# Experts with tokens as the moving operand: one store of y per item, zero rows behind each expert, and a conversion spread over seven items

## The chip, the cores and the metric

The kernel runs on one core of a Trainium2 chip. The metric is the device time of one execution in microseconds; lower is better. Five engines have a queue of their own: TensorE (PE in the rows; PEld are its weight loads), VectorE (DVE), ScalarE (ACT), GpSimd (POOL) and SyncE (SP), which computes nothing here and issues most DMAs. An instruction that waits holds up all that stand behind it on its engine.

## The reference

A chain of three parts, cut to what matters; arrays are fp32 but for w_in and w_out, which come as fp64:

```python
x = attention(q, k, v)               # 4608 tokens x 512
logits = norm(x) @ norm(emb).T / tau # 8 experts
idx = argmax(logits); gate = softmax(logits)[idx]
for e in range(8):
    m = idx == e
    out[m] = gate[m] * (relu(x[m] @ w1[e]) @ w2[e])   # 512 -> 1024 -> 512
h = out @ w_in                       # 512 -> 2048
y = (h * cos(h)) @ w_out             # 2048 -> 512
```

With these inputs the experts get 42, 708, 1, 145, 0, 2242, 1018 and 452 tokens.

## The kernel before

**Precision.** Each fp32 operand is split into a high and a low part (hi, lo), and a product is three matmuls: hi*hi, hi*lo, lo*hi. So each weight and each x needs a copy on ScalarE (hi) and a subtraction on VectorE or GpSimd (lo).

**Attention (0 to 186 us).** It makes x tile by tile, chooses the expert of each token, and GpSimd scatters the rows (with the gate as an extra column) into xv in DRAM, where each expert has a region of its own (`scatter`). `zero_rows` writes one block of zeros, the first 128 rows of each region, at step ZR = 8.

**Experts (to 898 us).** The work is a list of items: a wide item is up to 512 tokens of one expert, a narrow one up to 256. The table `tab` holds for each item its rows in xv, its columns in yv and the place of its weights; it is computed on VectorE during item 0 (`tables`). With these inputs there are 8 wide and 5 narrow items. Items 0 to 4 always run; wide items from 5 on and the narrow ones stand in nested If blocks on counts. Tokens are the moving operand: weights are loaded as 128x128 blocks and x, transposed, streams through.

An item has 16 steps k. Steps 0 to 7 are `gemm1(k)`: 12 matmuls into one of two banks, ScalarE's relu (L752) to hi, VectorE's L753 to lo. Steps 8 to 15 are halves of `gemm2`, whose result ScalarE copies to ys (L768). Beside them run for the next item: the loads of its x rows (`x_load`, L729, four of 257 KB), the multiplication by the gate (`gate`, L734, ScalarE), transposes on TensorE (`t_x`, L739) with XHI (L741, ScalarE) and XLO (L742, VectorE), its weights (`fetch`: four loads of 512 KB for w1 at L123 or w2 at L119, each after SP has read the address from `tab`), and their split (L126 ScalarE, L129 GpSimd or VectorE). The dictionaries FIRST, WIDE and NARROW say at which step each of these stands. At the item's end `y_store` writes ys to yv in four stores of 128 tokens (two in a narrow item); the first two of a wide item are declared disjoint, the others wait for the landing of the earlier ones.

**Conversion.** The feed-forward weights are converted from fp64 bits to fp32 in 32 pieces, each one load into one of two buffers craw, seven VectorE ops (L839 to L853) and one store wd<-co (L854) from the one buffer co; the sixth op, L849, is the first to write co. They are spread over items 0 to 4 by `conv`. In items 1 to 4 GpSimd also scatters each token's position to pv (`pos_scatter`, nine in each).

**Feed-forward (898 us to the end).** 9 groups of 512 tokens by 16 steps, with the converted weights read back and split (`f_load`, `f_split`), x read from yv (`x2_load`, `x2_split`), and the result scattered to the tokens' places. `prepare` does the first of these during the first narrow item.

All engines' orders are those in which the code is written.

## Time and profile before

| | us |
|---|---|
| median of 3 runs (1723.82 to 1728.4) | 1724.88 |
| the profiled execution's own time | 1710.43 |
| its span | 1708.5 |
| attention | 0 to 186 |
| item 0 | 216.1 to 284.2 |
| items 1 to 4 | 284.2 to 603.8 |
| wide items 5, 6, 7 | 603.8 to 757.5 |
| five narrow items | 757.5 to 898.3 |
| feed-forward | 898.3 to the end |

The stages' bounds are the starts of TensorE's first gemm of each. TensorE is busy for 1468.2 us of the span, VectorE for 924.8, ScalarE for 609.7, GpSimd for 490.9. The sum over the span tells little: the stages have different limits, so the windows by item, the waits and the timelines are read.

### The profile page before, as it was taken

The page shows a single profiled execution, that of the slowest core. Times are in us where ns is not written, and L with a number is a line of the kernel's source. Part 1 is how long each engine was busy: PE and PEld are TensorE (multiplying, and loading weights), DVE is VectorE, ACT ScalarE, POOL GpSimd, SP SyncE. Part 2 cuts the span into 40 slices and gives each one's busy share as a digit, 9 for nine tenths or more (in the row PEclk, how much of TensorE's full clock was granted, in tenths as well). Part 3 has the DMA queues.
Part 4 walks back from the last instruction along what each step waited for, and adds up shares of the span by engine and source line. Part 5 has one row for each costly group of instructions (what it writes and reads, how often), then busy time and mean ns, then how long its engine had stood idle before and what let it go on. Part 6 is the DMA issues. An engine that isn't in the chain of part 4 may idle for free. (4 is left out here: it accounts for less than half of the span.)

```text
span 1708.5 us, 20626 instructions
## 1 busy us (share of the span) xinstructions
PE 1468.2 (86%) x7480; PEld 1240.5 (73%) x7480; DVE 924.8 (54%) x1616; ACT 609.7 (36%) x1006; POOL 490.9 (29%) x378
## 2 busy tenths in 40 slices
PE   5999378384738579978998999999999999999996
PEld 4999256273636458868996788888888888888885
DVE  5788446373635431114446875656565656565653
ACT  5898324131212233326553332323232323232321
POOL 5576424242425224426333420202020202020200
PEclk9999689697969789999999999999999999999998
DMA  9973617464444554336663210101010101010000
GB/s 267 258 200 115 210 40 221 115 197 133 145 140 144 160 171 137 117 120 219 226 224 111 87 50 1 50 1 50 1 50 1 50 1 50 1 50 1 25 0 25
DMA packets 107073, 177.77 MB, mean 104 GB/s; under 512 B 16584, under 2 KB 54472, under 8 KB 106960
## 3 DMA queue, kind: packets, MB, share of 16 engines
q1 hardware_dynamic: 99888, 157.38, 30.6%
q0 software_dynamic: 6912, 18.94, 3.0%
q8 instruction: 62, 1.02, 0.2%
q14 instruction: 51, 0.42, 0.1%
q10 hardware_dynamic: 160, 0.02, 0.0%
HBM read 135.87 MB, written 40.43 MB: 103 GB/s over the span
## 5 line engine op out<-in xcount | busy, mean ns | idle before, releaser
L129 POOL TENSOR_TENSOR lo<-raw,hi 128x1024 fp32r<-128x1024 f32 x84 | 201.0, 2398 | 433.1 <-ACT hi L126 377.2
L749 PE MATMUL ph<-xhi,hi 128*128 128x512 f32 (+1 forms) x416 | 104.9, 377 | 139.9 <-DVE hb L753 116.7
L919 ACT ACTIVATE ys<-ph,quarter 128x512 f32<-128x512 f32 x144 | 99.0, 688 | 297.2 <-PE ph L911 297.2
L749 PEld LDWEIGHTS ph<-xhi,hi 128*128 128x128 f32 x416 | 73.7, 203 | 157.0 <-DVE hb L753 119.2
L935 PE MATMUL po<-fh,xhi 128*128 128x512 f32 x576 | 179.3, 392 | 3.2 <-DVE xhi L925 2.2
L935 PE MATMUL po<-hi,xhi 128*128 128x512 f32 x576 | 179.5, 391 | 0.4 <-DVE xhi L925 0.2
L922 ACT ACTIVATE ys<-ys 128x512 f32<-128x512 f32 x144 | 91.0, 632 | 227.5 <-DVE ys L921 227.5
L925 DVE TENSOR_TENSOR xhi<-ys,xhi 128x512 fp32r<-128x512 f32 x144 | 157.6, 1094 | 5.1
L923 DVE TENSOR_TENSOR ys<-ys,ph 128x512 f32<-128x512 f32 x144 | 99.2, 689 | 100.5 <-ACT ys L922 100.5
L920 DVE TENSOR_SCALAR co<-ys 128x512 f32<-128x512 f32 x144 | 62.7, 436 | 158.6 <-ACT ys L919 158.6
L764 PE MATMUL py<-ha,hi 128*128 128x256 f32 (+1 forms) x576 | 141.7, 338 | 2.0 <-ACT ha L752 1.9
L935 PEld LDWEIGHTS po<-fh,xhi 128*128 128x128 f32 x576 | 108.8, 189 | 27.3 <-DVE xhi L925 3.4
L935 PEld LDWEIGHTS po<-hi,xhi 128*128 128x128 f32 x576 | 108.1, 188 | 26.0 <-DVE xhi L925 3.4
L126 ACT ACTIVATE hi<-raw 128x1024 fp32r<-128x1024 f32 x108 | 112.2, 1053 | 12.9 <-SPq L998 8.7
L749 PE MATMUL ph<-xlo,hi 128*128 128x512 f32 (+1 forms) x416 | 103.8, 375 | 13.8 <-DVE xlo L742 13.8
L935 PE MATMUL po<-fl,xhi 128*128 128x512 f32 x288 | 112.6, 391 | 0.0
L935 PE MATMUL po<-lo,xhi 128*128 128x512 f32 x288 | 112.2, 390 | 0.0
L764 PEld LDWEIGHTS py<-ha,hi 128*128 128x128 f32 x576 | 97.2, 192 | 11.3 <-ACT ha L752 2.1
L921 DVE TENSOR_TENSOR ys<-ys,co 128x512 f32<-128x512 f32 x144 | 99.7, 693 | 4.9
L897 POOL TENSOR_TENSOR hb<-craw,hb 128x1024 fp32r<-128x1024 f32 x10 | 25.6, 2555 | 264.8 <-ACT hb L896 264.8
L749 PE MATMUL ph<-xhi,lo 128*128 128x512 f32 (+1 forms) x416 | 99.5, 363 | 2.4 <-POOL lo L129 2.4
L764 PE MATMUL py<-ha,lo 128*128 128x256 f32 (+1 forms) x288 | 95.9, 333 | 0.0
(201 smaller groups left out, 2862.0 us busy)
## 6 DMA issues: line engine op xcount, KB each, us to landing
raw<-in_moe_w_dram SPq DMA_DIRECT2D x116, 512.0 KB, 5.8
xr<-xv SPq DMA_DIRECT2D x46, 257.0 KB, 3.2
yv<-ys SPq DMA_DIRECT2D x42, 256.0 KB, 4.1
kraw<-in_k_dram SPq DMA_DIRECT2D x12, 768.0 KB, 9.2
vraw<-in_v_dram SPq DMA_DIRECT2D x8, 1152.0 KB, 7.6
craw<-yv SPq DMA_DIRECT2D x9, 1024.0 KB, 5.5
q<-in_q_dram SPq DMA_DIRECT2D x8, 1024.0 KB, 12.7
craw<-in_moe_w_in_dram SPq DMA_DIRECT2D x16, 512.0 KB, 4.3
```

What stands on the lines that cost most here:

```text
L126: nc.scalar.activation(HI[c], RAW[c], AF.Copy)
L129: eng.tensor_tensor(LO[c], RAW[c], HI[c].bitcast(F32), ALU.subtract)
L749: nc.tensor.matmul(p[:, 0:w], W[kk][:, f * 128:(f + 1) * 128], x[:, kk, 0:w], start=(c == 0), stop=(c == 3 * KC - 1))
L764: nc.tensor.matmul(p[:, 0:w], W[4 + f // 2][:, o:o + 128], h_at(f, m, w), start=(f == 0 and c == 0), stop=(f == FC1 - 1 and c == 2))
L897: nc.gpsimd.tensor_tensor(x[:, t, :], raw, x[:, s, :].bitcast(F32), ALU.subtract)
L919: nc.scalar.activation(u, p, AF.Identity, scale=1.0 / TWO_PI_EXACT, bias=quarter)
L920: nc.vector.tensor_scalar(nr, u, MAGIC, MAGIC, op0=ALU.add, op1=ALU.subtract)
L921: nc.vector.tensor_tensor(u, u, nr, ALU.subtract)
L922: nc.scalar.activation(u, u, AF.Sin, scale=TWO_PI)
L923: nc.vector.tensor_tensor(u, u, p, ALU.mult)
L925: nc.vector.tensor_tensor(gl, u, gh.bitcast(F32), ALU.subtract)
L935: nc.tensor.matmul(O[g][r], a[:, r * 128:(r + 1) * 128], wf(f, s, 1), start=(f == 0 and c == 0), stop=(f == FC2 - 1 and c == 2))
```

## The change

- **y_store:** one store of the whole item (512 or 256 columns), whose columns run on beyond the expert's end; the next item's store overwrites them. Each item needs one address instead of two or four.
- **Zero rows:** no longer the first rows of each region before the scatters, but 128 rows right behind each expert's last token, in eight stores with addresses from `basei`, issued by SP in item 0 (step 4) before the rows of item 1 are loaded. Rows of an item beyond its tokens point to them through `tab`.
- **w1:** the fetch for the item after next moves from the end of an item to step 14, except in item 0. For item 0 itself the w2 fetch moves behind the x rows. The first two items' row loads wait for the last eight scatters or zero stores issued ahead of them (`behind`).
- **Start:** the last chunk's routing, its scatters and the tables' set-up stand ahead of item 0's gates; the four gates come in a row, then four transposes in four banks. `tables` has 52 VectorE ops, 12 in each of steps 0 to 4 instead of steps 3 to 7.
- **Conversion:** two buffers co, and 3, 5, 5, 5, 5, 5, 4 pieces in items 0 to 6 instead of 32 in items 0 to 4. If item 5 or 6 does not run, Else branches do its pieces. In item 0 the pieces stand in steps 10 to 15.
- **Feed-forward's preparation:** spread over steps 0 to 15 of the first narrow item; f_split(1) stands right before the feed-forward loop; the buffers for split weights are laid out anew.

```diff
-    yv = dram.tile([128, KC, REG + 128], F32, name="yv")
+    yv = dram.tile([128, KC, NT + 512], F32, name="yv")
...
@@ -204,7 +212,6 @@
             lambda: V.tensor_scalar(m, k, float(REG), None, op0=ALU.mult),
             lambda: V.tensor_scalar(tab0[:, 0:4], row4, m[:, 0:1], None, op0=ALU.add),
             lambda: fetch(tab0, 0, 4, 0),
-            lambda: fetch(tab0, 0, 4, 1),
         ]
 
...
@@ -727,14 +738,16 @@
             for r in range(n):
                 row = nc.sync.value_load(t[i:i + 1, r:r + 1], min_val=0, max_val=E * REG - 128)
                 d = nc.sync.dma_start(xr[r], xv[bass.ds(row, 128), :])
+                if r == 0 and i < 2:
+                    behind(d, SENT[-8:])
                 if t is tab0:
                     tc.add_to_no_dep_group("xv_rows", d.ins)
...
-        def t_x(r):
-            p = bank(0, "ptx")
+        def t_x(r, b=0):
+            p = bank(b, "ptx")
             for kk in range(KC):
...
-        def y_store(i, n, k):
-            y = ys_at(n * 128)
-            for r in range(n):
-                col = nc.sync.value_load(tab[i:i + 1, 4 + r:5 + r], min_val=0, max_val=NT)
-                d = nc.sync.dma_start(yv[:, :, bass.ds(col, 128)], y[:, :, r * 128:(r + 1) * 128])
-                if r < 2 and n == 4:
-                    apart(f"y{k}", d)
+        def y_store(i, w):
+            col = nc.sync.value_load(tab[i:i + 1, 4:5], min_val=0, max_val=NT)
+            nc.sync.dma_start(yv[:, :, bass.ds(col, w)], ys_at(w))
+
+        def zero_rows(zeros):
+
+            for e in range(E):
+                row = nc.sync.value_load(basei[0:1, e:e + 1], min_val=e * REG, max_val=e * REG + NT)
+                d = nc.sync.dma_start(xv[bass.ds(row, 128), :], zeros)
+                apart("xv_rows", d)
+                SENT.append(d)
...
+        def item(i, w, conv=None, mid=None, when=None):
 
             n = w // 128
             w1c, w2c, on_dve, gates, txs = when
@@ -790,7 +809,9 @@
                 x_load(tab, i + 1, n)
             for k in range(16):
                 if k == 8:
-                    fetch(tab, i + 1, 8, 1)
+                    fetch(tab, i + 1, 5, 1)
+                if k == 14 and i:
+                    fetch(tab, i + 2, 5, 0)
                 if k < 8:
                     gemm1(k, w)
...
-                    conv(i, k)
+                    conv(k)
                 if k < 8:
                     for r in gates.get(k, ()):
                         gate(r)
-            fetch(tab, i + 2, 8, 0)
-            y_store(i, n, key)
-
-        FIRST = {11: (0,), 12: (1,), 13: (2,), 14: (3,)}, {1: (4, 5, 6, 7)}, (), {10: (0, 1), 12: (2, 3)}, {11: (0,), 12: (1,), 14: (2,), 15: (3,)}
+            if not i:
+                fetch(tab, 2, 5, 0)
+            y_store(i, w)
+
+        FIRST = {12: (0,), 13: (1,), 14: (2,), 15: (3,)}, {1: (4, 5, 6, 7)}, (1, 3), {11: (0,), 12: (1,), 13: (2,), 14: (3,)}, {12: (0,), 13: (1,), 14: (2,), 15: (3,)}
         WIDE = {8 + k: (k,) for k in range(4)}, {k: (4 + k,) for k in range(4)}, (), {4 + k: (k,) for k in range(4)}, {9: (0,), 11: (1,), 13: (2,), 15: (3,)}
...
+            o = co[j % 2]
...
+        PART = [3, 5, 5, 5, 5, 5, 4]
+        assert sum(PART) == 2 * FC2
+
+        def conv_part(i, k0, k1):
+
+            if i >= len(PART):
+                return None
+            j0, n = sum(PART[:i]), 7 * PART[i]
+            g = (x for j in range(j0, j0 + PART[i]) for x in conv_one(j))
+
+            def some(k):
+                for _ in range(n * (k - k0 + 1) // (k1 - k0) - n * (k - k0) // (k1 - k0) if k0 <= k < k1 else 0):
+                    next(g)
+            return some
...
         while todo and todo[0] < EARLY:
             scatter(todo.pop(0))
         x_load(tab0, 0, 4)
+        fetch(tab0, 0, 4, 1)
+        f1, f2 = route(NTILE - CHUNKS[-1], NTILE, const, lambda: bank(6, "pr"))
+        while todo:
+            scatter(todo.pop(0))
+        for f in f1:
+            f()
         for c in range(4):
             w_hi(c)
             w_lo(c, nc.vector)
+        for f in f2:
+            f()
+        for i in range(NTILE - CHUNKS[-1], NTILE):
+            scatter(i)
+        zeros = second_part()
+        late = tables(co[0], craw[0][:, 0, :])
         for r in range(4):
             gate(r)
-            t_x(r)
-        f1, f2 = route(NTILE - CHUNKS[-1], NTILE, const, lambda: bank(6, "pr"))
-        while todo:
-            scatter(todo.pop(0))
-        for f in f1[:-1]:
-            f()
-
-        late = []
+        for r in range(4):
+            t_x(r, (0, 3, 4, 5)[r])
 
         def mid0(n):
-            if n == 2:
-                f1[-1]()
-                for f in f2:
+            if n < 8:
+                for f in late[:LATE]:
                     f()
-                for i in range(NTILE - CHUNKS[-1], NTILE):
-                    scatter(i)
-                second_part()
-                late.extend(tables(co[0], craw[0][:, 0, :]))
-            if 2 < n < 8:
-                for f in late[:12]:
-                    f()
-                del late[:12]
-                if not late and not X1:
-                    X1.append(1)
-                    fetch(tab, 1, 8, 0)
+                del late[:LATE]
+                if not late and zeros is not None and not once:
+                    once.append(1)
+                    zero_rows(zeros)
                     x_load(tab, 1, 4)
+                    fetch(tab, 1, 5, 0)
                     conv_load(0)
                     conv_load(1)
 
-        X1 = []
-        item(0, 512, 0, conv, mid0, FIRST)
+        once = []
+        item(0, 512, conv_part(0, 10, 16), mid0, FIRST)
+        assert once
         for i in range(1, NW0):
...
         def more_wide(i):
-            with tc.If(nw > i):
-                item(i, 512, i, None, None, WIDE)
+            with tc.If(nw > i) as c:
+                item(i, 512, conv_part(i, 0, 16), None, WIDE)
                 if i + 1 < NWM:
                     more_wide(i + 1)
+            if i < len(PART):
+                with c.Else():
+                    for j in range(i, len(PART)):
+                        conv_part(j, 0, 1)(0)
 
...
         def prepare(k):
-            if k < 2:
-                x2_split(0, k)
-            if k == 2:
+            if k == 0:
+                f_load(0)
+            if k == 8:
+                x2_load(0)
+            if k == 10:
                 f_split(0)
+            if k in (13, 14):
+                x2_split(0, k - 13)
+            if k == 15:
                 for f in range(1, 4):
                     f_load(f)
-            if k == 6:
-                f_split(1)
 
         def more_narrow(j):
             with tc.If(nn > j) as c:
-                item(NROW + j, 256, 100 + j, None, (lambda k: prepare(k - 8) if k >= 8 else None) if not j else None, NARROW)
+                item(NROW + j, 256, None, None if j else prepare, NARROW)
                 if j + 1 < E:
                     more_narrow(j + 1)
             if not j:
                 with c.Else():
-                    for k in range(8):
+                    for k in range(16):
                         prepare(k)
 
         more_wide(NW0)
-        x2_load(0)
-        f_load(0)
         more_narrow(0)
...
         WF.extend((HI[c], LO[c]) for c in range(8))
-        WF.extend((piece(ffw, f"fh{f}"), piece(ffw, f"fl{f}")) for f in range(12, FC2))
+        WF.extend((piece(ffw, f"fh{f}"), piece(ffw, f"fl{f}")) for f in range(11, FC2 - 1))
+        WF.append(tuple(XLO[:, 2 * i:2 * i + 2, :].rearrange("p a n -> p (a n)") for i in range(2)))
+        f_split(1)
```

**SP, the end of item 1.** The rows stand between item 1 and item 2: raw are pieces of a later item's w1, yv<-ys the stores of y, xr the rows of x, wd the conversion's store. Before (the four rows of L773 and L774 stand there four times in a row, and so do those of L728 and L729):

```order
L123 DMA raw_109<-in_moe_w_dram 128x1024
L773 TENSOR_LOAD tab
L773 ISA x2
L774 REGISTER_ALU
L774 DMA yv<-ys 512x1x128
...
L728 TENSOR_LOAD tab
L728 ISA x2
L729 ISA
L729 DMA xr_101<-xv 128x514
...
L854 DMA wd<-co 128x512
```

And in the changed kernel:

```order
L124 DMA raw_110<-in_moe_w_dram 128x1024
L784 TENSOR_LOAD tab
L784 ISA x2
L785 REGISTER_ALU
L785 DMA yv<-ys 512x1x512
L739 TENSOR_LOAD tab
L739 ISA x2
L740 ISA
L740 DMA xr_102<-xv 128x514
...
L875 DMA wd<-co_2642 128x512
```

One store with one address stands where four did, the row loads come right behind it, and the w1 loads ahead of it are now issued at step 14.

**SP, in item 0, the rows of item 1.** tab_92 and tab_93 are the small table of item 0, tab that of all items; craw is the conversion's load. Before:

```order
L729 DMA xr_104<-xv 128x514
L116 TENSOR_LOAD tab
L116 ISA x2
L123 ISA
L123 DMA raw_106<-in_moe_w_dram 128x1024
...
L728 TENSOR_LOAD tab
L728 ISA x2
L729 ISA
L729 DMA xr_101<-xv 128x514
...
L826 DMA craw<-in_moe_w_in_dram 128x4x256
```

And in the changed kernel (the four rows of L790 and L791 stand there eight times):

```order
L120 DMA raw_114<-in_moe_w_dram 128x2x512
L790 TENSOR_LOAD basei
L790 ISA x2
L791 ISA
L791 DMA xv<-zeros 128x514
...
L739 TENSOR_LOAD tab
L739 ISA x2
L740 ISA
L740 DMA xr_102<-xv 128x514
...
L124 DMA raw_107<-in_moe_w_dram 128x1024
...
L848 DMA craw<-in_moe_w_in_dram 128x4x256
```

Eight zero stores now stand ahead of the rows of item 1, and the w1 fetch stands behind these rows instead of ahead of them.

## Rows read from the trace of the kernel before

**Rows 1.** The page's head and its busy totals.

```profile
span 1708.5 us, 20626 instructions
...
PE 1468.2 (86%) x7480; PEld 1240.5 (73%) x7480; DVE 924.8 (54%) x1616; ACT 609.7 (36%) x1006; POOL 490.9 (29%) x378
```

**Rows 2.** Windows: stretch, us, busy (instructions) by engine, granted clock, DMA share, GB/s.

```profile
216.10:284.20 68.10, 52.20 (x212) 41.27 (x212) 38.36 (x100) 19.41 (x29) 21.27 (x12) 0.87 0.39 135
284.20:361.60 77.40, 48.45 (x208) 39.02 (x208) 36.79 (x56) 19.14 (x28) 28.97 (x19) 0.82 0.59 143
361.60:603.80 242.20, 151.23 (x624) 121.48 (x624) 125.06 (x187) 57.57 (x84) 82.81 (x50) 0.80 0.49 148
603.80:662.60 58.80, 47.62 (x209) 38.77 (x209) 11.72 (x18) 19.15 (x28) 19.13 (x8) 0.91 0.47 148
662.60:709.10 46.50, 45.70 (x209) 37.65 (x209) 8.32 (x13) 19.15 (x28) 19.14 (x8) 1.00 0.43 136
757.50:898.30 140.80, 124.79 (x1000) 123.00 (x1001) 55.04 (x70) 76.56 (x124) 59.39 (x25) 0.96 0.64 212
836.00:860.00 24.00, 23.70 (x198) 23.49 (x198) 10.76 (x14) 14.25 (x25) 9.59 (x4) 1.00 0.66 213
```

**Rows 3.** Waits, whole span: who waits for what, sum in us, times, longest.

```profile
DVE co L849 <- DMA wd<-co: 133.3, 15, 28.9
...
ACT xr L734 <- DMA xr<-xv: 119.1, 14, 25.0
...
PE ph L749 <- DVE hb L753: 116.7, 6, 26.7
...
SPq L774 <- DMA yv<-ys: 123.8, 21, 19.4
```

**Rows 4.** Timeline of SP from 276 to 335 us: start, duration, instruction.

```profile
288.56 2.52 SPq L123 DMA_DIRECT2D raw<-in_moe_w_dram  x4
291.94 28.13 SPq L774 DMA_DIRECT2D yv<-ys  x4
320.91 3.85 SPq L729 DMA_DIRECT2D xr<-xv  x4
325.29 0.50 SPq L854 DMA_DIRECT2D wd<-co  x1
```

**Rows 5.** Timeline of VectorE, 276 to 365 us; in brackets the wait before.

```profile
330.72 0.69 DVE L849 SCALAR_TENSOR_TENSOR co<-craw,cb 128x512 f32<-128x512 uint32 x1 [27.48 <-DMA wd<-co]
```

**Rows 6.** Timeline of TensorE in the same item.

```profile
332.06 2.08 PE L749 MATMUL ph<-xhi,hi 128*128 128x512 f32 x4 [26.29 <-DVE hb L753]
```

**Rows 7.** DMA issues, 284 to 332 us: count, KB each, us to landing.

```profile
xr<-xv SPq DMA_DIRECT2D x4, 257.0 KB, 2.9
...
yv<-ys SPq DMA_DIRECT2D x4, 256.0 KB, 22.6
```

**Rows 8.** DMA issues, 605 to 640 us.

```profile
yv<-ys SPq DMA_DIRECT2D x4, 256.0 KB, 5.9
```

**Rows 9.** Lines of VectorE: count, busy, mean ns of one, idle before.

```profile
L841 DVE TENSOR_SCALAR ca<-ca 128x512 f32<-128x512 f32 x32 | 22.3, 698 | 1.0
```

**Rows 10.** Timelines of SP, ScalarE, TensorE and VectorE at the experts' start.

```profile
196.67 3.80 SPq L729 DMA_DIRECT2D xr<-xv  x4
...
205.71 0.72 ACT L734 ACTIVATE xr<-xr 128x512 f32<-128x512 f32 x1 [6.69 <-DMA xr<-xv]
...
206.48 1.11 PE L739 MATMUL ptx<-ident,xr 128*128 128x128 f32 x4 [19.29 <-ACT xr L734]
...
216.09 2.05 PE L749 MATMUL ph<-xhi,hi 128*128 128x512 f32 x4 [0.73 <-issue]
...
263.69 0.69 DVE L839 TENSOR_SCALAR ca<-craw 128x512 uint32<-128x512 uint32 x1 [10.69 <-DMA craw<-in_moe_w_in_dram]
```

**Rows 11.** Timelines of SP and TensorE, first narrow item and feed-forward's start.

```profile
755.04 9.51 SPq L774 DMA_DIRECT2D yv<-ys  x4
...
770.23 1.22 PE L749 MATMUL ph<-xhi,hi 128*128 128x256 f32 x4 [8.14 <-DVE ha L753]
...
898.30 1.17 PE L911 MATMUL ph<-hb,fh 128*128 128x512 f32 x4 [2.56 <-PEq L1014]
```

More of the change, by code (lines that the diff above doesn't have):

```diff
@@ L134, in apart, with behind @@
         tc.add_to_no_dep_group(group, dma.ins)
+    SENT, POSD = [], []
+    def behind(dma, others):
+        for o in others:
+            tc.add_manual_dep(dma.ins, o.ins.name, mybir.DependencyInfo(mybir.DependencyClass.Sync, mybir.DependencyReason.DATA))
     def route(n0, n1, sm, p):
@@ L511, in step @@
         def step(n):
-            if n == ZR:
-                zero_rows(zero)
             m, o = divmod(n, 9)
@@ L657, in tables @@
         V.tensor_scalar(nn, rel, 0.0, None, op0=ALU.is_gt)
-        V.tensor_scalar(key, cnt, 128.0, 100.0, op0=ALU.is_lt, op1=ALU.mult)
+        V.tensor_scalar(key, cnt, 512.0, 100.0, op0=ALU.is_lt, op1=ALU.mult)
+        V.tensor_scalar(one, cnt, 257.0, 100.0, op0=ALU.is_lt, op1=ALU.mult)
+        V.tensor_tensor(key, key, one, ALU.add)
         V.tensor_tensor(key, key, idx8[:, 0, :], ALU.add)
-        V.scalar_tensor_tensor(key, first_e, -200.0, key, op0=ALU.mult, op1=ALU.add)
+        V.scalar_tensor_tensor(key, first_e, -400.0, key, op0=ALU.mult, op1=ALU.add)
         V.tensor_tensor(less, key.unsqueeze(1).to_broadcast(wide), key.unsqueeze(2).to_broadcast(wide), ALU.is_lt)
@@ L712, in second_part @@
             moe2 = pool("moe2", 1)
-            WF.extend((piece(moe2, f"fh{f}"), piece(moe2, f"fl{f}")) for f in range(4))
+            WF.extend((piece(moe2, f"fh{f}"), piece(moe2, f"fl{f}")) for f in range(3))
             craw.append(moe2.tile([128, 2, 1024], F32, name="craw"))
-            co.append(moe2.tile([128, 512], F32, name="co"))
+            co.extend(moe2.tile([128, 512], F32, name=f"co{i}") for i in range(2))
+            zeros = moe2.tile([128, XW], F32, name="zeros")
+            nc.gpsimd.memset(zeros, 0.0)
+            return zeros
         def ys_at(w):
@@ L828, in conv_load, with conv_one @@
                 nc.sync.dma_start(t, w_out.bitcast(U32)[f * 128:(f + 1) * 128, :])
[L830 removed]
+        def conv_one(j):
             V = nc.vector
[L832 to L855 removed]
@@ L857, in experts_and_feed_forward @@
-        todo_conv = conv_ops()
-        def conv(i, k):
-            if not i:
-                n = 0 if k < 8 else 4 - k % 2
-            elif k < 8:
-                n = 2 + (k % 4 != 0)
-            else:
-                n = 3 + (k % 4 == 3) + (k == 15)
-            for _ in range(n):
-                next(todo_conv)
+            f, w = divmod(j, 2)
+            t = craw[0][:, j % 2, :].bitcast(U32).rearrange("p (n w) -> p w n", w=2)
+            L, Hw = t[:, 0, :], t[:, 1, :]
+            af, bf = bank(1, "ca"), bank(7, "cb")
@@ new lines, in conv_one @@
+            a, b = af.bitcast(U32), bf.bitcast(U32)
+            o = co[j % 2]
+            V.tensor_scalar(a, Hw, 0x7FFFFFFF, None, op0=ALU.bitwise_and)
+            yield
+            V.tensor_scalar(af, af, LOW, TOP, op0=ALU.max, op1=ALU.min)
+            yield
+            V.tensor_scalar(a, a, 3, 0x3FFFFFF8, op0=ALU.logical_shift_left, op1=ALU.bitwise_and)
+            yield
+            V.scalar_tensor_tensor(a, Hw, 0xC0000000, a, op0=ALU.bitwise_and, op1=ALU.bitwise_or)
+            yield
@@ new lines, in conv_one @@
+            V.tensor_scalar(b, a, 0xFF800000, None, op0=ALU.bitwise_and)
+            yield
+            V.scalar_tensor_tensor(o, L, 2.0 ** -52, bf, op0=ALU.mult, op1=ALU.mult)
+            if j + 2 < 2 * FC2:
+                conv_load(j + 2)
+            yield
+            V.tensor_tensor(o, af, o, ALU.add)
+            nc.sync.dma_start(wd[:, f, w * 512:(w + 1) * 512], o)
+            yield
+        PART = [3, 5, 5, 5, 5, 5, 4]
[9 more added lines that the diff above has]
+            return some
@@ L890, in x2_load @@
             nc.sync.dma_start(craw[0].rearrange("p a (b n) -> p (a b) n", b=2), yv[:, :, g * 512:(g + 1) * 512])
-            nc.sync.dma_start(POSF[:, g * 4:(g + 1) * 4], pv[g * 512:(g + 1) * 512, 0].rearrange("(r p) -> p r", p=128))
+            d = nc.sync.dma_start(POSF[:, g * 4:(g + 1) * 4], pv[g * 512:(g + 1) * 512, 0].rearrange("(r p) -> p r", p=128))
+            if g == 0:
+                behind(d, POSD[-8:])
         def x2_split(g, k):
@@ L1055, in attention_moe_ffn_kernel @@
         with ExitStack() as xes:
-            zero = pool("zp", 1, xes, side="right").tile([128, XW], F32, name="zero")
             xtp = pool("xtp", 18, xes, side="right")
-            nc.vector.memset(zero, 0.0)
             with ExitStack() as es:
-                phase_a(es, xtp, zero)
+                phase_a(es, xtp)
         psp.append(pool("ps", 1, space=PSUM))
```

78 lines of the change are left out of this document (29 added, 49 removed).

## The prediction

> **What bounds the kernel now.** The page gives the span and the totals [rows 1]: the profiled execution took 1710.43 us, 1.9 us more than its span, and 14.45 us less than the median of the runs shown (1724.88). The sum below is made against 1710.4; the median follows by adding 14.45. A difference under 0.3% (5 us) can't be told from none here.
>
> TensorE is busy 86% of the span, but that is a mean. The windows view by item [rows 2] shows where the rest lies. A wide item that nothing disturbs (the seventh, 662.60 to 709.10) takes 46.50 us with TensorE busy for 45.70 at a granted clock of 1.00. Items 1 to 5 do the same matmuls in 77.4, three times 80.7 (242.20/3) and 58.8 us, at a clock of 0.80 to 0.91. Against 46.5 each that is 145.9 us in these five items. Four narrow items take 140.80, of which the two undisturbed ones show 24.00 for one. From 898.3 the feed-forward part is bound by TensorE.
>
> The waits view [rows 3] names three waits of like size: VectorE waits 133.3 us at L849 for the store wd<-co, ScalarE 119.1 us at the gates L734 for the rows of x, TensorE 116.7 us at L749 for VectorE's L753. SP's own queue has 123.8 us at L774 on the stores of y. The timelines join them at the end of item 1. SP's four y stores begin at 291.94 and hold its queue for 28.13 us; only then, at 320.91, go out the row loads of the next item, and at 325.29 the conversion's store [rows 4]. VectorE stands at L849, since the one buffer co is not yet stored, for 27.48 us [rows 5]; the L753 behind it in VectorE's order is late, both banks of gemm1 stay full, and TensorE idles for 26.29 us [rows 6]. The lost time of this item, 77.4 - 46.5 = 30.9, is that gap and some 4.6 us of half clock behind it. ScalarE's gates wait for the same SP queue, up to 25.0 us in one go [rows 3]. So one queue blocks two engines, and either alone would stop TensorE.
>
> **The change, part by part.**
>
> *One store per item.* Four stores become one; their mutual waits for landing go. In SP's order the row loads stand right behind it. At 284 to 332 us a store of 256 KB took 22.6 us to land, a row load 2.9 [rows 7]; at the end of item 5, where no scatter runs, such a store took 5.9 [rows 8]. Bounds of one 1 MB store: from 5.9 to 22.6 us. I take about 10, nearer the low end, since the 22.6 holds the waits of a shared queue and three other stores. Rows that land 10 to 13 us into the item are in time: the first gate stands behind gemm1 step 4, some 5 x 2.9 = 14.5 us in (a step is 46.5/16), and the two banks give another step, so 17. The w1 fetch goes ahead to k = 14, so its 2 MB are no longer issued in the same moment as the store.
>
> *Two buffers co, seven items.* VectorE's op at L849 now waits for the store of two pieces ago. A piece is 7 ops of 0.70 us [rows 9], spread over some 9 us of an item; a store has that long to land before VectorE feels it. Items 1 to 4 hold 35 ops of the conversion where 45 were: 35 x 0.70 + 12 x 0.69 = 33 us of VectorE in 46.5, against 40 before. Items 5 and 6 get 35 and 28 ops, which they lacked; VectorE had only 11.72 and 8.32 us there [rows 2], so they stay covered by TensorE's 46.5.
>
> - Items 2 to 4: 242.2 to 3 x 48.0 = 144.0, **-98.2** (three of 46.5: -102.7; three like item 5 of before, 58.8: -65.8). The 1.5 us over the undisturbed one are for the position scatters, which stay.
> - Item 1: 77.4 to 52, **-25.4** (46.5: -30.9; 66: -11.4). It keeps the first scatter, and its predecessor still fetches w1 last.
> - Item 5: 58.8 to 47.5, **-11.3** (-12.3 to 0).
> - Items 6, 7: **0** (to +2 for the conversion).
>
> *The start and item 0.* Rows of x are issued at 196.67, behind the w2 fetch; the first gate runs at 205.71, nine us later, the transposes from 206.48, item 0's matmuls from 216.09 [rows 10]. With w2 behind the rows they land by about 201 (2.9 us alone, and the new wait for eight scatters); four gates of 0.72 in a row and transposes into four banks, no longer one after another through one bank, need some 5.5 us: start near 207, -9. But the tables are now ready about 17.5 us into item 0 (52 small ops in steps 0 to 4), and then SP issues eight zero blocks and waits for their landing before item 1's rows. A row load takes 0.95 us of SP (3.80/4) [rows 10]; with its value load I take 1.15, so 9.2 us, 3 us of landing, then rows, w1 and the conversion's first piece. That piece reaches VectorE about 48 us after the start, while its first op stands at k = 10, some 30 us in, ahead of the xlo of item 1. Before, the same op waited 10.69 us [rows 10]. TensorE can cover part; a stall of 10 stays, and item 0 becomes 63 instead of 68.1. Together item 1 begins at 270 instead of 284.2: **-14** (-22 without the stall; -2 if the new waits eat the earlier start).
>
> The zero block of the attention part (2 MB, in a stage that TensorE fills) goes: 0.
>
> *Narrow items.* At the start of this stretch SP holds 9.51 us in y stores, and TensorE idles for 8.14 [rows 11]. That stall goes with the single store; preparing the first group of the feed-forward part is spread to steps 0 to 15. 140.8 to 131, **-9.8** (five of 24.0: -20.8; +2 if the second transfer of the feed-forward group arrives late).
>
> *Feed-forward.* f_split(1) moves to just before the loop, one ScalarE copy and a GpSimd subtraction of some 2.4 us (19.14/8, [rows 2]), but the weights for it are loaded in the narrow item: **-2** (-5 to +3). Two Else branches add jumps for all engines. TensorE's queue held 2.56 us at the join at 898.30 [rows 11]; the added joins cost 0 to 5 us, of which 0 is taken, since TensorE has nothing in the new branches that is run.
>
> The Trainium skill ("Runtime: NRT & Kernel Launch", section Instruction fetch mechanics) says that a taken branch to code that is not prefetched makes the engine wait for a fetch of its instructions. The 2.56 us at the join agree with it; by that rule two more joins would add about 5 us, and the sum would be 1569.
>
> **Sum:** -98.2 - 25.4 - 11.3 - 14 - 9.8 - 2 = -160.7. 1710.4 - 160.7 = 1549.7, and with 14.45, **1564**. All good ends: -193.7, 1531. All bad ends: -65.8 - 11.4 - 0 + 2 - 2 + 2 + 3 = -72, 1653.
>
> **The rivals.**
>
> *A: the rows of x are still late.* w1 (2 MB), y (1 MB) and x (1 MB) meet at the item's boundary. At the 148 GB/s that the items move [rows 2] 4 MB take 28 us, of which two steps, 5.8, lie before the boundary: the rows would land 22 us in, 5 past the slack of 17, and half clock follows. Against it: the store has runs of 2 KB where it had 512 B, and a fetch and the store need not share every moment. Items 2 to 5 then take 58.8, as item 5 of before, item 1 66: -65.8 - 11.4 - 0 - 14 - 9.8 - 2 = -103, **1622**. [...] Chance 0.20.
>
> *B: every stall goes.* Items 1 to 5 at 46.5, narrow at 24: -102.7 - 30.9 - 12.3 - 14 - 20.8 - 2 = -182.7, **1542**; with the start's good end 1531. Speaks for it: the undisturbed items show that nothing else limits them. Against: the scatters stay. Chance 0.12.
>
> *C: item 0 gives nothing.* The zero blocks, issued late, hold SP so long that the stall is 20 to 26 us, not 10: +16, **1580**. Chance 0.10.
>
> *D: the change does not free SP.* If the four stores did not hold SP but what they waited for did (transfers slowed by the scatters, in which a landing took 22.6 us [rows 7]), VectorE and ScalarE wait as before, and only the start, the narrow items and -2 are won: -25.8, **1699**. Against it: item 5 has no scatter and lost only 12.3 us, and there too SP was held by its stores. Chance 0.03.
>
> *E: slower.* The 1 MB store lands so slowly that the rows behind it come 50 us into each item. Four stores and rows took until 324.8 + 2.9, some 43 us after the boundary, so it decides only if one store with long runs is slower than four in turn. A stall of 33 us makes an item 46.5 + 33 + 5 = 85; five of them 425 instead of 378.4, +46 and -26 elsewhere: **1745**. Chance 0.03.
>
> **How the numbers follow.** The forecast, sizes of the terms included, has 0.51; A 0.20, B 0.12, C 0.10, D 0.03, E 0.03; 0.01 for no change that can be told. The likeliest gives 1564, its own range from its terms is 1550 to 1590. To leave out no more than 2 in 10 the range takes in A and C at the top and half of B below: 1538 to 1625. Faster: 0.51 + 0.20 + 0.12 + 0.10 + 0.03 = 0.96; same 0.01; slower 0.03.
>
> **What the changed profile would show.** If right: waits of VectorE at the conversion's sixth op for wd<-co under 20 us in all; gates' waits for xr<-xv under 30; no gap of TensorE over 5 us in items 2 to 6; these items within 46.5 to 50 us at a clock near 1.00; item 0's matmuls from about 207 and item 1's from about 270, with one gap near step 12 of item 0. It is wrong if gates still wait over 5 us per item (A), if item 0's gap is over 15 (C), or if SP is still held over 15 us at the one store (D, E).

## The result and the profile after

The changed kernel takes 1584.39 us at the median of 4 runs (1581.51 to 1589.29), where the kernel before took 1724.72 beside it. The ratio is 0.9186, with a 95% interval of 0.9158 to 0.9213: 140 us less. The forecast was 1564, range 1538 to 1625.

The page of the changed kernel, its head and its busy totals:

```profile
span 1581.7 us, 20523 instructions
...
PE 1454.1 (92%) x7480; PEld 1231.9 (78%) x7480; DVE 933.0 (59%) x1623; ACT 609.6 (39%) x1006; POOL 485.1 (31%) x377
```

TensorE does the same work and is busy for 1454 us against 1468 [rows 1]; of the 126.8 us by which the span is shorter, some 113 are its idle time. The profiled execution took 1583.44 us, 0.95 under its median; that of before lay 14.45 under its own. So the two spans differ by 126.8 us and the medians by 140.3; no profile places the 13.5 us between these two numbers.

The windows view by item answers to [rows 2]; the columns are stretch, us, busy time (instructions) of PE, PEld, DVE, ACT and POOL, granted clock, DMA share, GB/s. The stretches are items 0 to 5 and the five narrow items:

```profile
208.05:275.45 67.40, 52.77 (x209) 42.43 (x209) 36.41 (x83) 18.46 (x28) 14.50 (x7) 0.84 0.50 169
275.45:349.07 73.62, 49.11 (x209) 39.52 (x209) 33.04 (x50) 19.92 (x29) 29.03 (x19) 0.81 0.76 150
349.07:404.93 55.86, 47.82 (x209) 38.90 (x209) 31.42 (x48) 19.04 (x28) 27.93 (x17) 0.94 0.80 185
404.93:453.41 48.48, 45.98 (x209) 37.55 (x209) 31.23 (x48) 19.04 (x28) 27.93 (x17) 1.00 1.03 209
453.41:506.19 52.78, 48.75 (x208) 39.59 (x208) 31.32 (x48) 19.26 (x28) 26.95 (x16) 0.94 0.89 218
506.19:552.68 46.49, 45.69 (x208) 37.63 (x209) 31.49 (x48) 19.16 (x28) 19.18 (x8) 1.00 0.68 213
...
647.60:774.35 126.75, 121.70 (x1000) 120.01 (x1001) 56.63 (x70) 75.55 (x123) 56.31 (x24) 1.00 0.75 235
```

Item 5 is now undisturbed, though it carries five pieces of the conversion; items 2 to 4 take 2 to 9 us more than it; item 1 has hardly gained. The waits view over the whole span answers to [rows 3]:

```profile
ACT xr L747 <- DMA xr<-xv: 51.2, 6, 26.6
...
PE ph L762 <- DVE hb L766: 36.0, 4, 23.8
...
DVE ca L860 <- DMA craw<-in_moe_w_in_dram: 26.1, 4, 17.0
```

TensorE's 116.7 us have become 36.0, of which one wait is 23.8; the gates' 119.1 have become 51.2; no row is left for VectorE on wd<-co, which had 133.3. The timelines of SP, ScalarE, VectorE and TensorE show the one wait, in item 1, and answer to [rows 4 to 6]. ScalarE's relu (L765) stands behind the gate that waits (L747), VectorE's L766 behind that relu, and TensorE behind L766:

```profile
281.59 5.88 SPq L124 DMA_DIRECT2D raw<-in_moe_w_dram  x4
288.25 0.68 SPq L785 DMA_DIRECT2D yv<-ys  x1
289.82 6.60 SPq L740 DMA_DIRECT2D xr<-xv  x4
...
316.85 0.72 ACT L747 ACTIVATE xr<-xr 128x512 f32<-128x512 f32 x1 [26.59 <-DMA xr<-xv]
...
318.09 0.69 DVE L766 SCALAR_TENSOR_TENSOR hb<-ph,hb 128x512 fp32r<-128x512 f32 x1 [25.29 <-ACT hb L765]
...
318.83 2.07 PE L762 MATMUL ph<-xhi,hi 128*128 128x512 f32 x4 [23.77 <-DVE hb L766]
```

SP is free: the store of y holds it for 0.68 us, where it held it for 28.13, and the rows go out right behind. They are issued 14.4 us into item 1, behind four loads of w1, and then they do not arrive: the first gate waits until 316.85, 27 us after the issue. The DMA issues of the same stretch (265 to 345 us, first row) and of an item without position scatters (599 to 625, second row), with KB of one load and us to landing, answer to [rows 7, 8]:

```profile
xr<-xv SPq DMA_DIRECT2D x4, 257.0 KB, 26.9
...
xr<-xv SPq DMA_DIRECT2D x4, 257.0 KB, 2.6
```

The same four loads take 26.9 us in the one place and 2.6 in the other. What is left of the stall is a slow transfer, no longer a blocked queue.

### The profile page after: what moved, and what is told of

It reads as the page before. It is cut to its first block, busy times and chain, and to the rows that moved or that the text cites. A ratio compares the mean times of both kernels' runs of the same rounds, so it can differ in the third digit from the quotient of the medians.

```text
span 1581.7 us, 20523 instructions
## 1 busy us (share of the span) xinstructions
PE 1454.1 (92%) x7480; PEld 1231.9 (78%) x7480; DVE 933.0 (59%) x1623; ACT 609.6 (39%) x1006; POOL 485.1 (31%) x377
## 4 chain that ended last, share of the span: by engine, by line
PE 39%; issue 5%; DVE 4%; ACT 1%; POOL 1%; DVEq 0%; POOLq 0%; ACTq 0%
PE ph L937 20%; PE po L961 20%; DVE xhi L951 2%; DVE ys L947 1%; DVE ys L949 1%; ACT ys L948 1%; DVE co L946 0%; DVE xhi L950 0%; POOL out_dram L972 0%; POOL ha L923 0%; ACT ha L922 0%; ACT ys L945 0%; DVEq L950 0%; POOLq L971 0%; POOLq L972 0%
## 5 line engine op out<-in xcount | busy, mean ns | idle before, releaser
L130 POOL TENSOR_TENSOR lo<-raw,hi 128x1024 fp32r<-128x1024 f32 x82 | 196.6, 2403 | 305.6 <-ACT hi L127 268.7
L961 PE MATMUL po<-fh,xhi 128*128 128x512 f32 x504 | 157.1, 392 | 2.8 <-DVE xhi L951 2.2
L762 PE MATMUL ph<-xhi,hi 128*128 128x512 f32 (+1 forms) x416 | 101.2, 366 | 53.7 <-DVE hb L766 36.0
L961 PEld LDWEIGHTS po<-fh,xhi 128*128 128x128 f32 x504 | 95.0, 188 | 24.4 <-DVE xhi L951 3.8
L961 PE MATMUL po<-fl,xhi 128*128 128x512 f32 x252 | 98.6, 391 | 0.0
L762 PE MATMUL ph<-xlo,hi 128*128 128x512 f32 (+1 forms) x416 | 98.4, 360 | 0.0
```

The costliest lines, as they stand in the source:

```text
L130: eng.tensor_tensor(LO[c], RAW[c], HI[c].bitcast(F32), ALU.subtract)
L762: nc.tensor.matmul(p[:, 0:w], W[kk][:, f * 128:(f + 1) * 128], x[:, kk, 0:w], start=(c == 0), stop=(c == 3 * KC - 1))
L961: nc.tensor.matmul(O[g][r], a[:, r * 128:(r + 1) * 128], wf(f, s, 1), start=(f == 0 and c == 0), stop=(f == FC2 - 1 and c == 2))
```

## The experiments

Each was profiled and timed against the kernel before on the same chip; the ratio and its 95% interval behind each time are against that kernel. The kernel before took 1721.08 to 1722.70 us there and 1724.72 beside the changed kernel, so a difference of a few us from the changed kernel's 1584.39 says nothing. Theory Q: the gain comes from SP's queue, which the four stores blocked. Theory S: what is left of the loss comes from GpSimd's position scatters, 36 of 128 words of 4 bytes. Theory V: it comes from the bytes that meet at an item's boundary.

**Four stores again.**

```diff
-            nc.sync.dma_start(yv[:, :, bass.ds(col, w)], ys_at(w))
+            for r in range(n):
+                col = nc.sync.value_load(tab[i:i + 1, 4:5], min_val=0, max_val=NT)
+                d = nc.sync.dma_start(yv[:, :, bass.ds(col + r * 128, 128)], ys_at(w)[:, :, r * 128:(r + 1) * 128])
+                if r < 2 and n == 4:
+                    apart(f"y{i}", d)
```

> The changed kernel with four stores of 128 columns per wide item (two per narrow) as before, the last two waiting for the first two; all else as changed. Theory Q: the gates wait for their rows in each of items 1 to 5 again; items 1 to 4 take 70 to 80 each, item 5 about 58, the narrow ones 135 to 141, the median 1650 to 1690. Theory S: with the two buffers co and the rest kept, only item 5 and the narrow items get slower by some 10 us each, the median is 1600 to 1615.

Measured: 1657.16 us, 0.9634 (0.9595 to 0.9672), 73 us over the changed kernel. Its windows of items 1 to 4 and of the narrow items:

```profile
271.00:345.06 74.06, 48.69 (x209) 39.24 (x209) 33.15 (x50) 20.03 (x29) 29.00 (x19) 0.82 0.64 149
345.06:413.26 68.20, 48.62 (x209) 39.45 (x209) 31.42 (x48) 19.03 (x28) 27.93 (x17) 0.85 0.62 150
413.26:478.94 65.68, 47.90 (x209) 38.90 (x209) 31.43 (x48) 19.03 (x28) 27.91 (x17) 0.87 0.61 156
478.94:550.13 71.19, 48.23 (x208) 39.18 (x208) 31.42 (x48) 19.04 (x28) 26.94 (x16) 0.83 0.53 161
...
700.88:840.39 139.51, 126.07 (x1000) 124.51 (x1001) 56.27 (x70) 75.72 (x123) 56.23 (x24) 0.95 0.67 214
```

The gates' wait over its whole span:

```profile
ACT xr L747 <- DMA xr<-xv: 111.6, 11, 27.5
```

And SP's timeline early in item 1:

```profile
283.42 26.16 SPq L787 DMA_DIRECT2D yv<-ys  x4
```

SP is held for 26 us again and the gates wait 111.6 us, with two buffers co and seven items kept. Items 2 to 4 take 205.1 us instead of 157.1, the narrow items 12.8 more. Theory Q holds by its median; items 2 and 3 stay under the 70 us that it gave, and item 5 takes 51.3, not 58. What four stores cost depends on the scatters beside them: SP is held for 21.5 to 30.3 us in items 1 to 4, where scatters run, and for 11.2 and 10.9 in items 5 and 6, which are only 4.8 and 4.2 us longer than with one store. Item 1 is as long with one store (73.6) as with four (74.1).

**The scatters later, in both kernels.** In the changed kernel, and the same move in the kernel before:

```diff
-            item(i, 512, conv_part(i, 0, 16), lambda k, i=i: pos_scatter((i - 1) * 9 + k) if k < 9 else None, WIDE)
+            item(i, 512, conv_part(i, 0, 16), lambda k, i=i: pos_scatter((i - 1) * 9 + k - 7) if k >= 7 else None, WIDE)
```

> The changed kernel with the nine position scatters of each of items 1 to 4 in steps 7 to 15 instead of 0 to 8, so that they begin after the rows of x should have landed. Theory S (the scatters slow every transfer beside them, and so the rows of x): the gap of 23.8 us in item 1 goes, item 1 takes 47 to 52 us instead of 73.6, items 2 to 4 together 140 to 148 instead of 157.1, the median falls by 30 to 40, to about 1550. Theory V (w1, y and x are too much for one boundary): item 1 stays within 70 to 76 and the median within 6 us of 1584. If the scatters only do their harm elsewhere, the next item's weights come late and a gap appears at steps 0 to 3 instead.

> The kernel before, with the same move of the position scatters to steps 7 to 15 and nothing else. Theory S as the whole cause (the four stores landed slowly only because of the scatters): items 1 to 4 fall to about 58.8 each, as item 5 has it without scatters, the median to about 1725 - 85 = 1640. Theory Q (the four stores in SP's queue and the one buffer co are the cause): items 1 to 4 stay above 70 each, the median above 1690.

Measured in the changed kernel: 1581.47 us, 0.9191 (0.9152 to 0.923), no difference. The windows of items 1, 2 and 5:

```profile
271.19:322.12 50.93, 47.83 (x209) 38.64 (x209) 33.05 (x50) 20.05 (x29) 28.08 (x18) 0.97 0.89 203
322.12:385.93 63.81, 51.28 (x208) 40.92 (x208) 31.32 (x48) 19.04 (x28) 27.94 (x17) 0.87 0.86 155
...
491.56:549.12 57.56, 48.53 (x209) 39.36 (x209) 31.32 (x48) 19.15 (x28) 19.17 (x8) 0.91 0.85 215
```

Item 1 falls to 50.9, as theory S had it; but item 2 rises to 63.8, and item 5, which has no scatter of its own but follows those now late in item 4, from 46.5 to 57.6. The sum of items 1 to 5 is 277.9, against 277.2. The loss moved with the scatters; it did not shrink, which is the third case of the expectation.

Measured in the kernel before: 1719.57 us, 0.9976 (0.9947 to 1.0005), unchanged; two of its waits:

```profile
DVE co L849 <- DMA wd<-co: 138.3, 14, 21.7
ACT xr L734 <- DMA xr<-xv: 82.7, 12, 16.1
```

Items 1 to 4 stay at 76.7 to 81.6 each, as theory Q had it; they take 316.6 us in all instead of 319.6, and item 5 takes 66.5 instead of 58.7. So the place of the scatters does not decide here either. But the four stores now hold SP for 10.8 to 19.8 us in items 1 to 4, where it was 23.7 to 28.1 before; SP's timeline in item 1, to be set beside [rows 4]:

```profile
296.89 10.82 SPq L774 DMA_DIRECT2D yv<-ys  x4
```

So scatters beside the stores made up much of SP's block, and a shorter block alone did not shorten the items. No run takes the scatters out of the kernel before; how much of its stall was theirs stays open.

**w1 behind the rows, in item 0; w1 at the end of every item.**

```diff
+            if i == 1:
+                fetch(tab, 2, 5, 0)
...
-            if not i:
-                fetch(tab, 2, 5, 0)
```

The `if` now stands behind item 1's x_load. The second kernel has the fetch at the end of each item instead:

```diff
-                if k == 14 and i:
-                    fetch(tab, i + 2, 5, 0)
...
-            if not i:
-                fetch(tab, 2, 5, 0)
+            fetch(tab, i + 2, 5, 0)
             y_store(i, w)
```

> The changed kernel with the w1 fetch that stands at the end of item 0 moved behind the store of y and the four row loads of item 1, one edit. Theory V: the rows no longer share the boundary with 2 MB, item 1 falls from 73.6 to 50 to 58 and the median by 15 to 23. Theory S: the rows are still slowed, item 1 stays above 66, the median falls by 0 to 8.

> The changed kernel with all w1 fetches at the end of the items, as before, in place of step 14. If w1, y and x in one moment cost the rows their time (the volume part of rival A), items 2 to 4 and 5 take 4 to 10 us more each, as item 1 has it with its w1 so placed; the median rises by 12 to 35. If the early fetch gives nothing, because the queue carries the same bytes either way, the median stays within 5 us.

Measured behind the rows: 1579.79 us, 0.9182 (0.9142 to 0.9222), no difference. Item 1 took 68.9, item 5 53.3, and the sum of items 1 to 5 was 278.8: again the loss only moved, which speaks for S and not for V.

Measured at the end of every item: 1616.92 us, 0.9381 (0.9333 to 0.9429), 32.5 over the changed kernel, within V's 12 to 35 for the median; by item it is 3.6, 15.3, 13.2 and 1.0 us more in items 2 to 5, where V had 4 to 10 in each. The windows of items 2 to 4:

```profile
344.68:404.10 59.42, 48.25 (x208) 38.94 (x208) 31.31 (x48) 19.15 (x28) 27.94 (x17) 0.91 0.79 173
404.10:467.86 63.76, 48.77 (x208) 39.52 (x208) 31.41 (x48) 19.05 (x28) 27.96 (x17) 0.87 0.64 161
467.86:533.80 65.94, 47.76 (x208) 38.82 (x208) 31.42 (x48) 19.19 (x28) 26.96 (x16) 0.87 0.68 156
```

The gates' wait over the span:

```profile
ACT xr L747 <- DMA xr<-xv: 95.2, 10, 26.8
```

In items 2 to 4 the rows are late where 2 MB of w1 are issued just ahead of them. Item 5, which has no scatter and takes 47.4 us with its w1 so placed, loses almost nothing.

**No scatters.**

```diff
         def pos_scatter(n):
...
+            pass
...
-                nc.gpsimd.tensor_copy(POS[:, g * 4:(g + 1) * 4], POSF[:, g * 4:(g + 1) * 4])
+                nc.gpsimd.tensor_copy(POS[:, g * 4:(g + 1) * 4], COLI[:, g * 4:(g + 1) * 4])
```

> The changed kernel without the 36 position scatters and the reads of pv; the feed-forward part takes the tokens' columns in their place, so that the output's rows stand in another order. Moving the scatters and moving the w1 fetch each took the gap out of item 1 and left the sum of items 1 to 5 at 277.2, 277.9 and 278.8 us. Theory S2 (the scatters slow the transfers wherever they stand, in all by a like amount): items 1 to 5 fall to 46.5 to 48 each, 233 to 240 in sum, the median to 1540 to 1550. Theory V2 (the five items simply move more bytes than the DMA engines carry, scatters or not): the sum stays above 265 and the median above 1570.

The kernel leaves out the positions and the feed-forward part's reads of pv as well, so its output rows stand in another order.

Measured: 1536.59 us, 0.8915 (0.8881 to 0.8949), 48 us under the changed kernel. The windows of items 1, 2 and 5:

```profile
270.88:321.85 50.97, 47.70 (x209) 38.53 (x209) 33.15 (x50) 19.94 (x29) 19.27 (x9) 0.97 0.70 241
321.85:368.38 46.53, 45.73 (x209) 37.63 (x209) 31.49 (x48) 19.17 (x28) 19.19 (x8) 1.00 0.66 220
...
461.43:507.95 46.52, 45.73 (x208) 37.62 (x208) 31.48 (x48) 19.17 (x28) 19.18 (x8) 1.00 0.67 215
```

The DMA issues over the whole span:

```profile
xr<-xv SPq DMA_DIRECT2D x46, 257.0 KB, 3.4
yv<-ys SPq DMA_DIRECT2D x8, 1024.0 KB, 5.7
```

Items 2 to 5 all take 46.5 with the same bytes of weights, rows and conversion, and a store of 1 MB lands in 5.7 us. The sum of items 1 to 5 is 237.1. So the scatters cost the changed kernel 40.1 us in these items, 1.1 us for each on the mean. Theory V2 falls. Not all of the 48 us are theirs: item 1 begins 4.6 us earlier (270.88 against 275.45), and no position scatter stands ahead of it; the feed-forward part is 2.5 us shorter. Item 1, where w1 is still issued just ahead of the rows, takes 4.5 us more than the others even without scatters.

**Nine in one go; the three edits together; eighteen in one go.** The first edit alone, then with the conversion's loads ahead of the zero stores (below) and w1 behind the rows, then the last two edits with 18 scatters in items 1 and 2:

```diff
+            item(i, 512, conv_part(i, 0, 16), lambda k, i=i: [pos_scatter((i - 1) * 9 + j) for j in range(9)] if k == 4 else None, WIDE)
...
+            item(i, 512, conv_part(i, 0, 16), lambda k, i=i: [pos_scatter((i - 1) * 18 + j) for j in range(18)] if k == 4 and i < 3 else None, WIDE)
```

> The changed kernel with the nine position scatters of an item in one go at step 4, behind GpSimd's four subtractions, instead of four single ones between these and five behind. In the trace of the changed kernel one scatter alone (396.67 us) is followed by some 8 us in which the DMA engines move a fifth of their packets, and eight near each other (412.19 to 428.10) by some 10. If the cost is one for each group (burst theory), items 1 to 4 lose 3 to 6 us each instead of 11.3 on the mean: the sum of items 1 to 5 is 245 to 260, the median 1553 to 1567. If it is one for each scatter, the sum stays at 272 to 282.

> Three edits together: the nine scatters in one go at step 4, the conversion's first loads ahead of the zero stores, and w1 of item 2 behind the rows of item 1. Alone the burst gave 1562.6. If the parts add, -4 to -9 for item 0 and -2 to -5 for item 1: 1549 to 1557. If the burst has already taken what w1 would give, 1554 to 1560.

> As the kernel with three edits, but the 36 scatters in two goes of 18, at step 4 of items 1 and 2. Burst theory (a cost for each group): items 3 and 4 take 46.5, items 1 and 2 lose as much as with nine; 8 to 15 us under the kernel with nine, 1538 to 1548. Cost for each scatter: items 1 and 2 lose twice as much, no gain, within 4 us. Against it: GpSimd is held for 18 x 1.26 = 23 us, so the subtractions of w1 come 12 us later; if that is too late, TensorE waits for lo at the first step of items 2 and 3.

Measured: 1562.57 us (0.9073, 0.9043 to 0.9102), 1562.31 (0.9069, 0.9031 to 0.9107), 1574.86 (0.9135, 0.9094 to 0.9176). The first two are faster than both kernels of this case by intervals that do not overlap; of the kernels here that compute everything they have the lowest medians, though the one with the conversion's loads first (1566.02, below) can't be told from them. The sums of items 1 to 5 are 263.4, 270.9 and 280.2 us. The three edits together miss both of their forecasts (1549 to 1557, 1554 to 1560): they are no faster than the burst alone. Eighteen in one go miss theirs too: against the 237.1 without scatters, each of two groups of eighteen costs some 21.5 us and each of four groups of nine 8.5. So the theory of a fixed cost for a group falls, and one cost for each scatter does not fit either. Nine in one go save 14 us in these items. The gates wait 14.9 us in all instead of 51.2, and VectorE waits 64.1 for the conversion's loads instead of 26.4: these are slowed in place of the rows. Whether the saving comes from the place, step 4, or from the grouping is not shown, since this edit changes both; later steps without grouping saved nothing. The windows of items 2 and 3 with 18 in one go:

```profile
321.64:387.29 65.65, 47.48 (x209) 38.63 (x209) 31.38 (x47) 19.16 (x28) 36.81 (x28) 0.87 0.90 161
387.29:454.06 66.77, 48.81 (x208) 39.60 (x208) 34.19 (x52) 19.17 (x28) 29.22 (x13) 0.85 0.81 206
```

A wait of VectorE in the timeline of item 2, and the one of TensorE behind it:

```profile
336.69 0.69 DVE L860 TENSOR_SCALAR ca<-craw 128x512 uint32<-128x512 uint32 x1 [19.04 <-DMA craw<-in_moe_w_out_dram]
...
340.23 2.08 PE L762 MATMUL ph<-xlo,hi 128*128 128x512 f32 x4 [17.38 <-DVE xlo L755]
```

The conversion's loads are now too late for TensorE: VectorE waits 19 us for one, and xlo behind it holds TensorE for 17. GpSimd's late subtractions, the doubt that was named, did not show.

**One buffer co; five items.**

```diff
-            o = co[j % 2]
+            o = co[0]
```

```diff
-        PART = [3, 5, 5, 5, 5, 5, 4]
+        PART = [4, 7, 7, 7, 7]
...
+        item(0, 512, conv_part(0, 8, 16), mid0, FIRST)
```

> The changed kernel with one buffer co for the conversion again. If VectorE's wait at the sixth op was only a follower of SP's blocked queue (theory Q), one store of y suffices: the median rises by 0 to 6 us. If the second buffer carried a part of the gain of its own (the forecast's count), VectorE waits for wd<-co again in the items with scatters, 10 to 20 us each, items 1 to 4 take 5 to 15 us more each, the median rises by 15 to 50.

> The changed kernel with the conversion's pieces as 4, 7, 7, 7, 7 over items 0 to 4 (seven pieces, 49 ops and 5.25 MB in an item, where five, 35 ops and 3.75 MB stood). Theory V2: 1.5 MB more in each of items 1 to 4 at 185 to 209 GB/s cost 7 to 8 us each, less what items 5 and 6 no longer carry (they have no gap to give back): the median rises by 25 to 35. Theory Q with VectorE's own count (49 x 0.70 + 12 x 0.69 = 43 us in 46.5): the median rises by 0 to 12.

Measured: 1594.26 us (0.927, 0.923 to 0.9309) and 1634.49 (0.95, 0.947 to 0.9529), 10 and 50 us over the changed kernel. Two rows of waits, the first with one buffer, the second with five items:

```profile
DVE co L870 <- DMA wd<-co: 40.8, 13, 11.3
```

```profile
DVE ca L860 <- DMA craw<-in_moe_w_in_dram: 65.4, 5, 29.4
```

The 10 lie between the two theories: of VectorE's 133.3 us on wd<-co in the kernel before, 40.8, about a third, come back with the one buffer while SP is free. In these profiles the sum of items 1 to 5 rises by 14.0 and the experts start 4.7 us earlier, so 10 is no sharp number. The 50 are more than either theory gave. Seven pieces are the 49 VectorE ops that an item of the kernel before has. The 6 MB that move into items 1 to 4 take some 32 us at about 190 GB/s, an estimate from the windows of these items; the sum of items 1 to 5 rose by 41, item 0, with one piece more, by 7. The rest is not explained.

**The conversion's loads ahead of the zero stores.**

```diff
+                    conv_load(0)
+                    conv_load(1)
                     zero_rows(zeros)
                     x_load(tab, 1, 4)
                     fetch(tab, 1, 5, 0)
-                    conv_load(0)
-                    conv_load(1)
```

> The changed kernel with the conversion's first two loads ahead of the eight zero stores in item 0's SP order, one edit. VectorE waits 17.0 us there for the first load, and TensorE 7.3 us at the transposes behind it. If SP's order of the zero stores is the cause (the forecast's step on item 0), VectorE's wait falls under 3 us, TensorE's 7.3 us go, item 0 takes 58 to 62 instead of 67.4, and the median falls by 4 to 9. Rival: the 7.3 us pass to another wait, since the rows of item 1 are later by two issues (1.6 us) and must land anyway; then item 0 stays above 65 and the median within 3 us.

Measured: 1566.02 us, 0.9088 (0.9049 to 0.9126), 18 us under the changed kernel. The windows of items 0 and 1:

```profile
202.28:262.68 60.40, 50.83 (x209) 40.61 (x209) 34.72 (x80) 18.50 (x28) 15.62 (x8) 0.91 0.51 178
262.68:331.22 68.54, 49.74 (x209) 39.84 (x209) 35.06 (x53) 20.05 (x29) 27.96 (x17) 0.88 0.75 178
```

Item 0 loses 7.0 us, as expected. The start of the experts is 5.8 us earlier, which the edit doesn't touch: in these profiles it lies at 202.3 to 208.1 without a pattern, so not all of the 18 us belong to the edit; and this profiled execution (1573.14 us) lies 7 above its own median, so the two profiles place only some 10 of them. In the kernel with three edits item 0 fell to 58.3, but item 1 took 8 us more than with the burst alone: what was won ahead was given back.

## Why the prediction was right, and where not

The mechanism was right in its main part: SP's queue, blocked by four stores, made the gates and VectorE late, and one store frees it (73 us when undone, 26 us of SP held again). What it left out is that the scatters lengthen the block and the landings of the rows behind it. The median, 1584.39, lies inside the range, 20 us above the forecast. Of the signs that the forecast named, two came: VectorE no longer waits for wd<-co, and the store holds SP for 0.68 us. Three did not. The gates wait 51.2 us where under 30 was said, and in items 1, 2 and 4 over 5 us in one go, which the forecast named as the sign of rival A. Items 2 and 4 take more than 50 us. And TensorE has a gap of over 5 us in item 2; its timeline there:

```profile
375.65 2.08 PE L762 MATMUL ph<-xhi,hi 128*128 128x512 f32 x4 [7.24 <-DVE hb L766]
```

By the forecast's terms, from the two profiles:

| term | forecast | bounds | measured |
|---|---|---|---|
| items 2 to 4 | -98.2 | -102.7 to -65.8 | -85.1 |
| item 1 | -25.4 | -30.9 to -11.4 | -3.8 |
| item 5 | -11.3 | -12.3 to 0 | -12.3 |
| items 6, 7 | 0 | 0 to +2 | 0 |
| start and item 0 | -14 | -22 to -2 | -8.8 |
| narrow items | -9.8 | -20.8 to +2 | -14.1 |
| feed-forward | -2 | -5 to +3 | -2.9 |
| sum (measured: of the unrounded terms) | -160.7 | -193.7 to -72 | -126.8 |

- **The mis-sized step** is the landing of the store and the rows: "I take about 10, nearer the low end", and rows "10 to 13 us into the item". The rows landed 26.9 us after their issue in item 1, 18.0, 9.4 and 20.8 in the next three (the DMA issues of these items), and 2.6 where no scatter runs; in item 1 that is 41 us into the item. The forecast had the 22.6 us of [rows 7] before it and put them down to the shared queue and the other stores; it gave the scatters 1.5 us an item, and they cost 40 in items 1 to 5. Rival D named them, for the whole of the stall, with 0.03; in item 1 they were most of it (73.6 us with them, 51.0 without, 74.1 with them and four stores).
- **Rival A**, the rows late at the boundary, was half right in its effect: two of its items came (1 and, in part, 2). Its cause, the bytes that meet, counts for much only together with the scatters: w1 at the end of each item costs 32.5 us with them, while item 5 without them stays at 47.4 and item 1 without them loses 4.5. The forecast gave the early w1 no price of its own.
- **Item 0.** The start came at 208.05 where 207 was forecast. VectorE waited 17.0 us for the conversion's first load and TensorE 7.3 behind it, where 10 was forecast; a second gap of 6.6 us at 227.77 was not named. It stands behind the tables' small ops on VectorE, four of which took 1.8 to 2.4 us each and the others under 0.5; why is open. So the zero stores went out 24.7 us into the item and not 17.5, and item 0 took 67.4, not 63.
- **Two buffers and seven items** were right in direction. The forecast counted 45 conversion ops in an item of the kernel before; its code has 49 in items 1 to 4, so VectorE had 43 us to do there and not 40. Undone one at a time, four stores cost 73, five items 50, the late w1 32.5 and one buffer 10; together that is more than the 140 gained. So the parts overlap; that each alone brings back waits that the others share is argued, not shown.
- **Narrow items.** They are five, where the forecast once writes four; and its 24.00 us for an undisturbed one is the width of the window that was asked. The starts of TensorE's gemms give 24.3 to 24.5 in both kernels, so all five undisturbed would be some 122 us, not 120. Of the 14.1 us gained, four stores bring back 12.8.
- **Rival B.** Its "1531 with the start's good end" should be 1534; 1531 takes the feed-forward part's good end as well.
- **Feed-forward.** The join holds TensorE 2.75 us at 774.35, where it held it 2.56 [rows 11], and item 7 takes 48.4 as before: the added branches cost nothing there. The 5 us more that the forecast worked out beside the Trainium skill's rule on taken branches ("Runtime: NRT & Kernel Launch", section Instruction fetch mechanics) did not come.
- **The median.** The forecast added the 14.45 us by which the profiled execution of before lay under its median. That of the changed kernel lies 0.95 under its own. This hid 13.5 of the 33.9 us by which the sum was off, and that was luck.

## What to carry to other kernels

When a store, a load and a wait share one engine's queue, count the instructions with waits ahead of the one that others need: fewer stores can be worth far more than their bytes. When the queue is freed, look at what slowed the transfers in it, by the landing times of the same load with and without each neighbour. The loss that small scattered writes bring moved with them here, and issuing nine in one go at step 4 saved a third of it; before moving such writes, take them out once, to see what they cost.

## What the runs showed of the hardware

A scatter of 128 words of 4 bytes costs the transfers that SP issued beside it far more than its 512 bytes. One alone, in GpSimd's timeline of the changed kernel:

```profile
396.67 0.98 POOL L797 DMA_INDIRECT pv<-GT,COLI  x1 [0.18 <-issue]
```

And three windows of 8 us, the first some 3 us behind it; the next scatters are issued at 412.19, 415.80 and 419.41:

```profile
400.00:408.00 8.00, 7.20 (x34) 5.76 (x33) 5.06 (x8) 1.10 (x3) 0.00 (x0) 1.00 1.11 114
408.00:416.00 8.00, 8.00 (x37) 6.62 (x36) 5.90 (x9) 4.62 (x6) 5.98 (x4) 1.00 0.93 351
416.00:424.00 8.00, 8.00 (x37) 6.51 (x35) 4.05 (x7) 2.17 (x4) 7.58 (x5) 1.00 1.23 152
```

The DMA engines count as busy in all three windows (1.11, 0.93 and 1.23), but carry 114 and 152 GB/s behind scatters and 351 in the one between. In the kernel without scatters a window as busy (374 to 382 us, 0.98) carries 331. Why is not settled: no run varied the size of the scattered words. The Trainium skill ("DMA: Bandwidth & Descriptors", section Specifications) says that below 512 B a DMA engine does a read-modify-write. No run here shows whether that is what slows the loads. The Trainium skill ("DMA: Bandwidth & Descriptors", section Issuing engines are not separate DMA queues) says that DMAs started by SP and by GpSimd run on the same 16 DMA engines and interleave there. The loads that SP issued landed in 26.9 us beside GpSimd's scatters and in 2.6 without them, which agrees.
